# Attention and SwiGLU block on one core: the last unit's row sums on TensorE, the last output tiles split into FFN and attention, and a DMA ring in the scheduler's model

## The chip, the cores and the metric

One core of one Trainium2 chip. The metric is the device time of one execution in microseconds (us). All runs told here are of the fast state; a run also has a mean granted TensorE clock (1.000 is full speed).

Engine names: PE is TensorE's matmul, PEld its weight load, DVE is VectorE, ACT is ScalarE, POOL is GpSimd, SP issues the DMAs. "L1230" is a line of the kernel in question; lines of helpers collect many uses.

## The reference, cut to what matters

```python
def reference(A_x, A_wqkv, A_wo, B_x, B_w1, B_w3, B_w2):   # x: 1 x 2048 x 512, 32 heads of 16, F = 1792
    xn = _layernorm(A_x)
    q, k, v = split_heads(xn @ A_wqkv)
    p = softmax(q @ k.T * 16 ** -0.5)                       # 32 heads x 2048 x 2048 exponentials
    h = silu(xn @ B_w1) * (xn @ B_w3)
    return A_x + (p @ v) @ A_wo + h @ B_w2
```

## The kernel before: the parts that matter

The kernel writes its own schedule. While the program is built, a small simulator runs on the host with one clock per engine; whenever an engine is free *in the model*, the next piece of work is chosen and appended to that engine's instruction list. On the chip each engine runs its list in order, and semaphores keep it correct. So a wrong duration in the model does not make a wrong result by itself; it makes a wrong **order**, and an engine then stands before an instruction whose input is late while later work in its list could have run.

```python
class _Sched(_Prog):
    ...
    def dma(self, fn, reads=(), writes=(), kb=64, name="", eng="sp"):
        op = _Prog.dma(self, fn, reads, writes, name, eng)
        return self._time(op, op.deps, 0.06, 1.9 + kb / 200.0)     # 0.06 us to issue, no queueing
```

The work is 32 units (4 blocks of 512 queries x 8 groups of 4 heads). A unit has 64 score matmuls of 512 columns; most pairs of them are exponentiated by ACT (line `f_PT`, 128x1024), the others by a chain of DVE instructions (line `f_xd`). Dense tiles (Q, K, V, FFN, OUT) fill the gaps on PE. When a unit's P times V is complete, its sums of rows are inverted and spread over the partitions by DMA; the normalized result, `onorm`, is what the output tile (OUT) multiplies by A_wo:

```python
def unit_end(u, o):
    # e0: DVE copies U <- PSUM;  e1: DMA gathers the sums Lc <- U (and moves half of U)
    # e2: DVE Rc = 1 / Lc;       e3: DMA Rrow <- Rc
    # e4: 4 DMAs R <- Rrow, each row broadcast to 16 partitions
    # e5: onorm = U * R   (POOL; DVE for the last unit)
    ...
```

The output tile of the last query block had two parts: the FFN product with three of four attention groups (it can start only once the third group's onorm is there), and the last group by itself:

```python
def tile_OUT(tg, part):
    ...
    if part not in (2, 4): ... FFN groups ...
    for g in range(NP):
        if part == 1 and g == NP - 1 or part == 2 and g < NP - 1 or part == 3:
            continue
        ... attention group g ...
```

## Time and profile before

| | before |
|---|---|
| time, median of 3 runs (range) | 855.96 us (852.74 to 856.73) |
| span of the profiled run | 853.8 us |
| ACT busy, PE busy, DVE busy | 93%, 90%, 86% |
| ACT idle, 0 to 60 us | 24.1 us |
| last exponential to the end | 22.66 us |

Three lines of the page of the kernel before. The first has the busy time of each engine; the others are tenths of busy time of ACT, and tenths of the granted PE clock, in 40 slices of the span.

```profile
...
PE 764.9 (90%) x8693; PEld 214.3 (25%) x8693; DVE 738.3 (86%) x975; ACT 797.3 (93%) x893; POOL 30.9 (4%) x41
...
ACT  4589999999999999999999999999996999999990
...
PEclk9899999999999999999999999999996999999996
...
```
ACT is the bound nearly everywhere: it is at 9 in all slices but the first three (4, 5, 8), one in the middle (6) and the last (0). So time can only come back where ACT is idle. The stage table of the same kernel (from:to in us, length, busy us of each engine with the number of instructions, then the granted clock, the DMA share and GB/s):

```profile
...
core 0: us, PE busy (x) PEld busy (x) DVE busy (x) ACT busy (x) POOL busy (x), PEclk, DMA share, GB/s
26.00:40.00 14.00, 7.84 (x94) 2.94 (x90) 7.58 (x19) 7.78 (x9) 1.76 (x4) 0.87 0.64 184
40.00:60.00 20.00, 18.53 (x222) 5.46 (x214) 7.10 (x13) 15.63 (x17) 0.00 (x0) 0.92 0.06 14
640.00:644.00 4.00, 1.94 (x26) 0.41 (x18) 2.72 (x3) 2.88 (x4) 1.61 (x1) 0.98 0.26 13
644.00:650.00 6.00, 6.00 (x44) 1.03 (x46) 3.12 (x4) 3.36 (x4) 0.00 (x0) 0.50 0.06 22
650.00:657.00 7.00, 7.00 (x52) 1.20 (x44) 3.41 (x5) 4.83 (x5) 0.00 (x0) 0.50 0.06 19
831.14:853.80 22.66, 7.00 (x107) 2.72 (x99) 6.13 (x14) 0.00 (x1) 0.00 (x0) 0.66 0.28 41
...
```
Read it in three places. **Start**: from 40 to 60 us PE is busy 18.53 of 20 us, ACT has 4.4 us idle and DVE works only 7.1 us. **Dent**: from 644 to 657 us the clock is 0.50, PE is busy all the time, and ACT is idle 4.8 of 13 us (called a dip of the clock from here on); just before, in 640 to 644, PE was busy only 1.94 of 4 us. **Tail**: 22.66 us in which nothing is left for ACT.

Who stood waiting for whom (us in total, how often, the longest one), from the list of waits of the kernel before:

```profile
...
DVE f_onorm L1820 <- DMA f_R<-f_Rrow: 7.2, 1, 7.2
...
PE ps L1556 <- DMA f_KT<-f_stg: 6.0, 1, 6.0
...
PE ps L1230 <- POOL f_onorm L1820: 2.1, 1, 2.1
...
```
The first line is in the tail, the second in the start (at 33 to 39 us), the third is the one that precedes the dent. The tail itself, from the timeline (start, length, engine, line, operation, output and input, count; in brackets how long the engine was idle and what it waited for):

```profile
...
828.22 2.92 ACT L1594 ACTIVATE f_PT<-ps 128x1024 bf16<-128x1024 f32 x3
...
831.74 0.69 DVE L1778 COPY f_U<-ps 128x512 f32<-128x512 f32 x1 [3.42 <-PE ps L1760]
...
832.46 0.62 SPq L1785 DMA_DIRECT2D f_Lc<-f_U  x1
...
835.75 0.63 SPq L1805 DMA_DIRECT2D f_Rrow<-f_Rc  x1
...
837.80 2.42 SPq L1810 DMA_DIRECT2D f_R<-f_Rrow  x4
844.21 0.69 DVE L1820 TENSOR_TENSOR f_onorm<-f_U,f_R 128x512 bf16<-128x512 f32 x1 [7.22 <-DMA f_R<-f_Rrow]
...
844.96 1.90 PE L1230 MATMUL ps<-f_wo,f_onorm 128*32 128x512 bf16 x16 [8.72 <-DVE f_onorm L1820]
...
845.63 2.49 DVE L1428 TENSOR_TENSOR f_xn_sb<-ps,f_wkv 128x512 bf16<-128x512 f32 x4 [0.72 <-PE ps L1230]
...
846.35 3.10 SPq L1434 DMA_DIRECT2D out_dram<-f_xn_sb  x4
```
Follow the hops: last exponential ends at 831.14, U is copied, the sums are gathered by DMA (832.5 to 834.4), inverted, sent to Rrow (835.75 to 837.8), spread by four DMAs whose issue alone takes 2.4 us and which land at 844.1; DVE idles 7.22 us for them. PE, having stood still, runs the last 16 matmuls in 1.90 us.

### The profile page before, as it was taken

The numbers are of one execution on the slowest core, as the hardware profiler recorded it, in microseconds if no ns is written. First come the engines' busy times: TensorE is split into PE (matmuls) and PEld (weight loads), VectorE is DVE, ScalarE is ACT, GpSimd is POOL, SyncE is SP. The second block draws the span as 40 slices with busy tenths as digits, with TensorE's granted clock in tenths as the row PEclk, the third lists the DMA queues.
The fourth block names the chain that finished last, engine by engine and source line by source line (L and its number), as shares of the span: only waits on it lengthen the run. The fifth ranks groups of instructions, "written<-read, shape, count | busy, mean of one in ns | idle before, by whom it ended". The sixth has DMA issues, their size and how long they took to land.

```text
span 853.8 us, 20404 instructions
## 1 busy us (share of the span) xinstructions
PE 764.9 (90%) x8693; PEld 214.3 (25%) x8693; DVE 738.3 (86%) x975; ACT 797.3 (93%) x893; POOL 30.9 (4%) x41
## 2 busy tenths in 40 slices
PE   4689999998999999899999999899998989989892
PEld 2222222222222222222222222222221222222230
DVE  5548988999979989998999899998985899989982
ACT  4589999999999999999999999999996999999990
POOL 2100000000000000000000000000000000000000
PEclk9899999999999999999999999999996999999996
DMA  8503313233221223333211333333120432231222
GB/s 316 159 14 39 51 43 55 35 54 45 40 21 36 44 38 45 40 51 45 27 19 30 45 44 45 45 46 45 10 31 21 70 39 31 42 40 7 18 28 42
DMA packets 90580, 40.48 MB, mean 47 GB/s; under 512 B 72560, under 2 KB 86640, under 8 KB 90480
## 3 DMA queue, kind: packets, MB, share of 16 engines
q1 hardware_dynamic: 90480, 39.09, 29.4%
q8 instruction: 70, 1.15, 0.6%
q14 instruction: 30, 0.25, 0.1%
HBM read 22.81 MB, written 2.10 MB: 29 GB/s over the span
## 4 chain that ended last, share of the span: by engine, by line
ACT 64%; PE 21%; DVE 8%; DMA 5%; issue 1%; SPq 1%; POOL 0%; DVEq 0%; POOLq 0%
ACT f_PT L1594 61%; PE ps L1230 9%; PE ps L1556 7%; PE ps L1760 5%; ACT f_th L1366 3%; DVE f_xd L1646 2%; DMA f_KT<-f_stg 1%; DVE f_xd L1692 1%; DMA f_wkv<-in_A_wqkv_dram 1%; DMA f_R<-f_Rrow 1%; DVE f_xd L1706 1%; DVE f_xd L1685 1%; DVE f_hT L1380 1%; DMA f_QT<-f_stg 1%; DMA f_Rrow<-f_Rc 0%
## 5 line engine op out<-in xcount | busy, mean ns | idle before, releaser
L1594 ACT ACTIVATE f_PT<-ps 128x1024 bf16<-128x1024 f32 x819 | 769.2, 1095 | 19.4 <-PE ps L1556 18.6
L1556 PE MATMUL ps<-f_QT,f_KT 32*128 32x512 bf16 x2048 | 327.8, 388 | 40.4 <-ACT f_PT L1594 26.3
L1646 DVE TENSOR_SCALAR f_xd<-ps 128x1024 int16<-128x1024 f32 x205 | 250.3, 1221 | 32.1 <-PE ps L1556 24.2
L1760 PE MATMUL ps<-f_PT,f_Vaug 128*17 128x512 bf16 (+1 forms) x1638 | 223.1, 389 | 1.3 <-DVE f_xd L1701 0.6
L1760 PE MATMUL ps<-f_xd,f_Vaug 128*32 128x512 bf16 (+1 forms) x1230 | 178.9, 388 | 5.7 <-DVE f_xd L1692 2.2
L1556 PEld LDWEIGHTS ps<-f_QT,f_KT 32*128 32x128 bf16 x2048 | 82.0, 91 | 351.8 <-ACT f_PT L1594 301.1
L1230 PE MATMUL ps<-f_xnT,f_w 128*32 128x512 bf16 x1792 | 150.6, 383 | 8.0 <-DVE f_t L1370 5.9
L1692 DVE TENSOR_TENSOR f_xd<-f_xd 128x2048 bf16<-128x2048 bf16 (+1 forms) x112 | 126.2, 1127 | 0.0
L1701 DVE TENSOR_SCALAR f_xd<-f_xd 128x2048 int16<-128x2048 int16 (+1 forms) x112 | 74.1, 661 | 2.5
L1685 DVE TENSOR_SCALAR f_xd<-f_xd 128x2048 int16<-128x2048 int16 (+1 forms) x112 | 74.3, 663 | 2.1 <-PE ps L1760 0.2
L1706 DVE TENSOR_SCALAR f_xd<-f_xd 128x2048 int16<-128x2048 int16 (+1 forms) x112 | 74.2, 662 | 2.2
L1230 PE MATMUL ps<-f_w,f_hT 128*32 128x512 bf16 x896 | 75.8, 382 | 0.2 <-DVE f_wkv L1420 0.2
L1760 PEld LDWEIGHTS ps<-f_PT,f_Vaug 128*17 128x17 bf16 (+1 forms) x1638 | 54.2, 91 | 83.3 <-issue 69.1
L1760 PEld LDWEIGHTS ps<-f_xd,f_Vaug 128*32 128x32 bf16 (+1 forms) x1230 | 43.2, 92 | 56.1 <-issue 27.4
L1230 PEld LDWEIGHTS ps<-f_xnT,f_w 128*32 128x32 bf16 x1792 | 39.6, 95 | 59.2 <-issue 48.4
L1820 POOL TENSOR_TENSOR f_onorm<-f_U,f_R 128x512 bf16<-128x512 f32 x15 | 21.4, 1429 | 742.5 <-DMA f_R<-f_Rrow 647.9
L1370 DVE SCALAR_TENSOR_TENSOR f_t<-f_th,ps 128x512 bf16<-128x512 f32 x56 | 38.2, 682 | 8.8 <-ACT f_th L1366 8.6
L1380 DVE SCALAR_TENSOR_TENSOR f_hT<-f_t,ps 128x512 bf16<-128x512 bf16 x56 | 38.1, 681 | 6.1 <-PE ps L1230 4.9
L1366 ACT ACTIVATE f_th<-ps 128x512 f32<-128x512 f32 x56 | 38.9, 695 | 0.0
L1230 PE MATMUL ps<-f_wo,f_onorm 128*32 128x512 bf16 x256 | 24.9, 432 | 12.4 <-DVE f_onorm L1820 8.7
L1230 PEld LDWEIGHTS ps<-f_w,f_hT 128*32 128x32 bf16 x896 | 21.3, 95 | 19.9 <-issue 11.5
L1778 DVE COPY f_U<-ps 128x512 f32<-128x512 f32 x32 | 21.9, 684 | 4.1 <-PE ps L1760 4.0
(50 smaller groups left out, 210.1 us busy)
## 6 DMA issues: line engine op xcount, KB each, us to landing
f_w<-in_B_w_dram SPq DMA_DIRECT2D x112, 128.0 KB, 2.4
f_R<-f_Rrow SPq DMA_DIRECT2D x128, 32.0 KB, 4.0
f_KT<-f_hT SPq DMA_DIRECT2D x6, 512.0 KB
f_KT<-f_stg SPq DMA_DIRECT2D x32, 64.0 KB, 2.0
f_QT<-f_stg SPq DMA_DIRECT2D x32, 64.0 KB
f_U<-f_U SPq DMA_DIRECT2D x64, 32.0 KB, 2.0
f_xr<-in_A_x_dram SPq DMA_DIRECT2D x16, 128.0 KB
out_dram<-f_xn_sb SPq DMA_DIRECT2D x16, 128.0 KB, 3.3
```

The source lines that it names most:

```text
L1230: ins = e.matmul(bank(bk)[32 * i:32 * i + 32, 0:ncols], make_lhsT(i), rhs_ap, start=start, stop=stop, tile_position=(0, 32 * i))
L1366: q = P.op("act", lambda e: e.activation(th[:, ss, :], bank(bk), ACTF.Tanh, scale=0.5), reads=[("ps", bk)], writes=[("th", ss)], dur=a_cos ...
L1370: q2 = P.op("dve", lambda e: e.scalar_tensor_tensor(t1[:, ss, :], th[:, ss, :], 1.0, bank(bk), ALU.add, ALU.mult), reads=[("th", ss), ("ps ...
L1380: q = P.op("dve", lambda e: e.scalar_tensor_tensor(hT[:, fc, :], t1[:, ss, :], 0.5, bank(bk), ALU.mult, ALU.mult), reads=[("t1", ss), ("ps ...
L1556: ins = e.matmul(bank(b), l_, r_, start=True, stop=True, tile_position=(rp, 0))
L1594: q = P.op("act", lambda e: e.activation(PT[:, s_, :], ps[:, b0 * 512:(b0 + 2) * 512], ACTF.Exp, scale=ASC, bias=ABIAS), reads=[("ps", b0) ...
L1646: q = P.op("dve", lambda e: e.tensor_scalar(dsl[:, ys, 1024 * c:1024 * c + 1024], ps[:, 4 * 512:6 * 512], 0.0, 32767.0, ALU.max, ALU.min), ...
L1685: P.op("dve", lambda e: e.tensor_scalar(dsl[:, NY + m_, 0:n], y, 0x7F, 0x3F00, ALU.bitwise_and, ALU.bitwise_or), reads=[("ds", ys)], write ...
L1692: q_ = P.op("dve", lambda e: e.tensor_tensor(t_ap.bitcast(BF16), y.bitcast(BF16), t_ap.bitcast(BF16), ALU.mult), reads=[("ds", ys)], write ...
L1701: q_ = P.op("dve", lambda e: e.tensor_scalar(g_ap, y, -352.0, 0.0, ALU.add, ALU.max), reads=[("ds", ys)], writes=[("ds", NY + NM + g_)] + ...
L1706: q_ = P.op("dve", lambda e: e.tensor_scalar(y, y, 0x7F80, None, ALU.bitwise_and), reads=[], writes=[("ds", ys)], dur=s_cost(n), name="e")
L1760: ins = e.matmul(bank(PV)[32 * j:32 * j + (17 if g % 2 == 0 else 32), :], v_, p_, start=s0, stop=s1, tile_position=(0, 32 * j))
```

## The change

The intent, in four pieces. (1) The **last** unit's sums are taken by fp32 matmuls from the copied U, inverted out of PSUM by DVE, and spread by 16 small fp32 matmuls with an identity. (2) The last pair's onorm comes in two halves, each masked, A (the first unit of the pair, still by DMA, multiplied by DVE while the scores still run) and B (by TensorE), and the last OUT becomes FFN alone (early) plus attention alone (five groups, late). Odd tiles add the FFN sum by an fp32 matmul with the identity, so that ACT can take their last copy. (3) The DMA model: 0.56 us per issue, one ring that all DMAs share at 270 KB per us, 1.5 us to land. (4) Small matters: constants made on POOL, bank 5 kept free at the end, four open tiles at the end instead of two.

```diff
-    def dma(self, fn, reads=(), writes=(), kb=64, name="", eng="sp"):
+    def dma(self, fn, reads=(), writes=(), kb=64, name="", eng="sp", rate=270.0):
         op = _Prog.dma(self, fn, reads, writes, name, eng)
-        return self._time(op, op.deps, 0.06, 1.9 + kb / 200.0)
+        self._time(op, op.deps, 0.56, 0.0)
+        self.ring = max(self.ring, op.end) + kb / rate
+        op.end = self.ring + 1.5
+        return op
 ... (constants idf, sell, msk) ...
 def tile_OUT(tg, part):
+            gr = {2: ats + [og(NP - 1, ON_B, ("ON", qc, "B"))], 3: ffn, 4: ats, 0: ffn + ats}[part]
+            by_pe = part == 2 and ts % 2 == 1
+            if by_pe:
+                groups.insert(1, (lambda e, bk: e.matmul(bank(bk), idf[:, :], osum[:, ts, :], start=False, stop=False),
+                                  [("idf",), ("osum", ts)], None, 0.95))
 ...
             for ts in range(4):
-                bg.append(tile_OUT(sc * 4 + ts, 1 if sc == NQC - 1 else (3 if sc < 3 else 0)))
+                bg.append(tile_OUT(sc * 4 + ts, 3))
 ...
 def unit_end(u, o):
-                if h:
-                    eng = "dve" if u == NU - 1 else "pool"
+                if h or u == NU - 2:
+                    eng = "dve" if u == NU - 2 else "pool"
 ...
+        def last_end(o):
+            # ACT: U <- PSUM;  PE: 4 matmuls U.T @ sell (the sums);  DVE: reciprocal from PSUM
+            # PE: 16 matmuls, Rc broadcast x identity (the spread);  DVE: onorm B = U * mask * PSUM
```

More of the change, by code (lines that the diff above doesn't have):

```diff
@@ L149, in __init__ @@
         self.t = 0.0
+        self.ring = 0.0
     def _time(self, op, deps, dur, tail):
@@ L1072, in _plan_fast @@
         fm = sb("fm", [1, 1], FP32)
+        idf = sb("idf", [128, 128], FP32)
+        sell = sb("sell", [128, 4], FP32)
+        msk4 = sb("msk4", [128, 4], FP32)
+        msk = sb("msk", [128, 2], FP32)
         def bank(b):
@@ L1206, in _plan_fast, with tail_consts, tail_masks @@
         P.post("dve", wv_check, ready=60.0, prio=4)
+        def tail_consts():
+            P.op("pool", lambda e: e.memset(idf[:, :], 1.0), writes=[("idf",)], dur=0.2)
+            P.op("pool", lambda e: e.affine_select(idf[:, :], idf[:, :], [[1, 128]], ALU.is_equal, 0.0,
+                                                   base=0, channel_multiplier=-1),
+                 reads=[("idf",)], writes=[("idf",)], dur=0.4)
+            P.op("pool", lambda e: e.memset(sell[:, :], 1.0), writes=[("sell",)], dur=0.1)
+            P.op("pool", lambda e: e.affine_select(sell[:, :], sell[:, :], [[-32, 4]], ALU.is_equal, 0.0,
+                                                   base=-15, channel_multiplier=1),
+                 reads=[("sell",)], writes=[("sell",)], dur=0.2)
+            P.op("pool", lambda e: e.memset(msk4[:, :], 1.0), writes=[("msk4",)], dur=0.1)
+            P.op("pool", lambda e: e.affine_select(msk4[:, :], msk4[:, :], [[-32, 4]], ALU.is_ge, 0.0,
+                                                   base=-16, channel_multiplier=1),
+                 reads=[("msk4",)], writes=[("msk4",)], dur=0.2)
+            P.op("pool", lambda e: e.affine_select(msk4[:, :], msk4[:, :], [[32, 4]], ALU.is_ge, 0.0,
+                                                   base=31, channel_multiplier=-1),
+                 reads=[("msk4",)], writes=[("msk4",)], dur=0.2)
+            P.post("dve", tail_masks, ready=P.free["pool"] + _LAT, prio=4)
+        def tail_masks():
+            P.op("dve", lambda e: e.tensor_reduce(msk[:, 1:2], msk4[:, :], AX.X, ALU.add), reads=[("msk4",)],
+                 writes=[("msk", 1)], dur=0.1)
+            P.op("dve", lambda e: e.tensor_scalar(msk[:, 0:1], msk[:, 1:2], -1.0, 1.0, ALU.mult, ALU.add),
+                 reads=[("msk", 1)], writes=[("msk", 0)], dur=0.1)
+        P.post("pool", tail_consts, ready=100.0, prio=4)
         def load_w13(idx):
@@ L1396, in tiles_FFN, with og @@
                     _T("Y%d_%d" % (sc, fc), mk(1), evac_u, cond=lambda: ("G%d_%d" % (sc, fc)) in done)]
+        ON_B = (NQC * NP) % NON
         def tile_OUT(tg, part):
             qc, ts = divmod(tg, 4)
-            gr = []
-            if part not in (2, 4):
-                for fc in range(FC):
-                    gr.append((lambda i, fc=fc: hT[:, fc, ts * 128 + 32 * i:ts * 128 + 32 * i + 32], w2[:, fc, :],
-                               [("hT", fc), ("w2",)], None))
-            for g in range(NP):
-                if part == 1 and g == NP - 1 or part == 2 and g < NP - 1 or part == 3:
-                    continue
-                gr.append((lambda i, g=g: onorm[:, (qc * NP + g) % NON, ts * 128 + 32 * i:ts * 128 + 32 * i + 32], wo[:, g, :],
-                           [("ON", (qc * NP + g) % NON)] + [("wor", j_, h_) for j_ in range(4) for h_ in range(2)],
-                           lambda g=g: have(("ON", qc, g))))
+            def og(g, slot, key):
+                return (lambda i: onorm[:, slot, ts * 128 + 32 * i:ts * 128 + 32 * i + 32], wo[:, g, :],
+                        [("ON", slot)] + [("wor", j_, h_) for j_ in range(4) for h_ in range(2)],
+                        lambda: have(key))
+            ffn = [(lambda i, fc=fc: hT[:, fc, ts * 128 + 32 * i:ts * 128 + 32 * i + 32], w2[:, fc, :],
+                    [("hT", fc), ("w2",)], None) for fc in range(FC)]
+            ats = [og(g, (qc * NP + g) % NON, ("ON", qc, g)) for g in range(NP)]
+            gr = {2: ats + [og(NP - 1, ON_B, ("ON", qc, "B"))], 3: ffn, 4: ats, 0: ffn + ats}[part]
+            by_pe = part == 2 and ts % 2 == 1
@@ L1412, in tile_OUT @@
             groups = []
             for k, (lh, rh, rd, cd) in enumerate(gr):
-                groups.append((lambda e, bk, lh=lh, rh=rh, k=k: col_groups(lh, rh, D)(e, bk, k == 0, k == len(gr) - 1),
-                               rd, cd, DG))
+                groups.append((lambda e, bk, lh=lh, rh=rh, k=k: col_groups(lh, rh, D)(
+                    e, bk, k == 0, k == len(gr) - 1), rd, cd, DG))
+            if by_pe:
+                groups.insert(1, (lambda e, bk: e.matmul(bank(bk), idf[:, :], osum[:, ts, :], start=False, stop=False),
+                                  [("idf",), ("osum", ts)], None, 0.95))
@@ L1417, in evac, with e1 @@
             def evac(bk, o, rel):
-                def e1():
-                    if part in (1, 3):
+                def e1(eng="dve"):
+                    if part == 3:
                         q = P.op("dve", lambda e: e.tensor_tensor(osum[:, ts, :], bank(bk), xr[:, ts % 2, :], ALU.add),
@@ L1427, in e1 @@
                     other = osum[:, ts, :] if part in (2, 4) else xr[:, ts % 2, :]
-                    q = P.op("dve", lambda e: e.tensor_tensor(osb[:, ts, :], bank(bk), other, ALU.add),
+                    if by_pe and eng == "act":
+                        fn = lambda e: e.activation(osb[:, ts, :], bank(bk), ACTF.Identity)
+                    elif by_pe:
+                        fn = lambda e: e.tensor_copy(osb[:, ts, :], bank(bk))
+                    else:
+                        fn = lambda e: e.tensor_tensor(osb[:, ts, :], bank(bk), other, ALU.add)
+                    q = P.op(eng, fn,
                              reads=[("ps", bk), ("osum", ts) if part in (2, 4) else ("xr", ts % 2)],
                              writes=[("osb", ts), ("xn", ts)],
-                             dur=d_cost(512))
+                             dur=d_cost(512) if eng == "dve" else a_cost(512))
                     rel(q)
@@ L1436, in e1 @@
                            ready=q.end + _LAT, prio=1)
-                P.post("dve", e1, ready=o.end + _LAT, prio=1, cond=lambda: part in (2, 4) or ("xr", tg) in done)
+                if by_pe:
+                    P.post2({"dve": lambda: e1("dve"), "act": lambda: e1("act")}, ready=o.end + _LAT,
+                            prios={"dve": 2, "act": 1})
+                else:
+                    P.post("dve", e1, ready=o.end + _LAT, prio=1, cond=lambda: part in (2, 4) or ("xr", tg) in done)
             def cond():
-                if part in (2, 4):
+                if part == 4:
                     return have(("OSUM", tg), ("ON", qc, NP - 1))
+                if part == 2:
+                    return have(("OSUM", tg)) and st["pos"] >= NR
                 if not have(*[("hT", qc, fc) for fc in range(FC)]):
                     return False
-                if part in (1, 3) and qc > 0 and ("OUT", (qc - 1) * 4 + ts) not in done:
+                if part == 3 and qc > 0 and ("OUT", (qc - 1) * 4 + ts) not in done:
                     return False
@@ L1447, in cond @@
                     return have(*[("KTm", NG - 1, i_) for i_ in range(NQC)])
-                g_need = NP - 2 if part == 1 else NP - 1
-                return have(("ON", qc, g_need))
+                return have(("ON", qc, NP - 1))
             def start():
@@ L1516, in dense_banks @@
             if st["pos"] >= NR and st["n_exp"] >= NR:
-                return [6, 0, 1, 2, 3, 4, 5]
+                return [6, 0, 1, 2, 3, 4]
             if st["early"]:
@@ L1795, in ec @@
                     l_check(0, NU - 1, 1)
-                elif u == NU - 1:
-                    done["accb"] = l_check(NU - 1, NU, 2).end + _LAT
             def e2():
@@ L1819, in e5 @@
                 on = (u // 2) % NON
+                if u == NU - 2:
+                    q = P.op(eng, lambda e: e.scalar_tensor_tensor(onorm[:, on, :], U[:, 0, :], msk[:, 0:1], R[:, :],
+                                                                   ALU.mult, ALU.mult),
+                             reads=[("Uc",), ("msk", 0)] + [("R", j_, h_) for j_ in range(4) for h_ in range(2)],
+                             writes=[("ON", on)], dur=0.68)
+                    done[("ON", qc, pi)] = q.end + _LAT
+                    return
                 q = P.op(eng, lambda e: e.tensor_tensor(onorm[:, on, :], U[:, 0, :], R[:, :], ALU.mult),
@@ L1825, in e5, with copy, col_sums, f @@
                 done[("e5", u // 2)] = q.end
+            if u == NU - 1:
+                return last_end(o)
             P.post("dve", e0, ready=o.end + _LAT, prio=0, cond=lambda: u < 2 or h == 1 or ("e5", u // 2 - 1) in done)
+        def last_end(o):
+            u = NU - 1
+            qc = NQC - 1
+            def copy():
+                q = P.op("act", lambda e: e.activation(U[:, 1, :], bank(PV), ACTF.Identity), reads=[("ps", PV)],
+                         writes=[("Ut",)], dur=a_cost(512), name="U")
+                st["tail"] = (q.end + _LAT, col_sums)
+            def col_sums():
+                def f(e):
+                    for k in range(4):
+                        ins = e.matmul(bank(5)[:, 4 * k:4 * k + 4], U[:, 1, 128 * k:128 * k + 128], sell[:, :],
+                                       start=True, stop=True)
+                    return ins
+                q = P.op("pe", f, reads=[("Ut",), ("sell",)], writes=[("ps", 5)], dur=0.6, name="S")
+                P.post("dve", inv, ready=q.end + _LAT, prio=0)
+            def inv():
+                q = P.op("dve", lambda e: e.reciprocal(Rc[:, :], bank(5)[:, 0:16]), reads=[("ps", 5)],
+                         writes=[("Rc",)], dur=0.25)
+                st["tail"] = (q.end + _LAT, spread)
+                P.op("dve", lambda e: e.tensor_copy(Lc[:, u, :], bank(5)[:, 0:16]), reads=[("ps", 5)],
+                     writes=[("Lc", u)], dur=0.1)
+                done["accb"] = l_check(NU - 1, NU, 2).end + _LAT
+            def spread():
+                def f(e):
+                    for k in range(4):
+                        for j in range(4):
+                            ins = e.matmul(bank(PV)[32 * j:32 * j + 32, 128 * k:128 * k + 128],
+                                           Rc[:, 4 * k + j:4 * k + j + 1].to_broadcast((128, 32)), idf[:, :],
+                                           start=True, stop=True, tile_position=(0, 32 * j))
+                    return ins
+                q = P.op("pe", f, reads=[("Rc",), ("idf",)], writes=[("ps", PV)], dur=1.1, name="S")
+                P.post("dve", norm_b, ready=q.end + _LAT, prio=0)
+            def norm_b():
+                q = P.op("dve", lambda e: e.scalar_tensor_tensor(onorm[:, ON_B, :], U[:, 1, :], msk[:, 1:2], bank(PV),
+                                                                 ALU.mult, ALU.mult),
+                         reads=[("Ut",), ("ps", PV), ("msk", 1)], writes=[("ON", ON_B)], dur=0.68)
+                done[("ON", qc, "B")] = q.end + _LAT
+            P.post("act", copy, ready=o.end + _LAT, prio=0)
@@ L1832, in start_tile @@
             banks = [b for b in dense_banks() if bank_free[b] <= P.t and not any(a.bank == b for a in active)]
-            if not banks or len(active) >= 2:
+            if not banks or len(active) >= (4 if st["pos"] >= NR else 2):
                 return
@@ L1844, in start_tile @@
                 tl = None
-                cand = bg[:3] + [x for x in bg[3:] if x.name[0] == "O" and x.name.endswith("_4")]
+                cand = bg[:4 if st["pos"] >= NR else 3] + [x for x in bg[3:] if x.name[0] == "O" and x.name.endswith("_4")]
                 if cand and any(z[0] == 0 for z in crit[:4]):
@@ L1893, in fin @@
         def fin():
-            o = P.op("pe", lambda e: e.matmul(bank(PV)[:, 0:3], ones_t[:, :], accb[:, :], start=True, stop=True),
-                     reads=[("ones_t",)] + [("acc", i) for i in range(3)], writes=[("ps", PV)], dur=0.1)
+            o = P.op("pe", lambda e: e.matmul(bank(5)[:, 0:3], ones_t[:, :], accb[:, :], start=True, stop=True),
+                     reads=[("ones_t",)] + [("acc", i) for i in range(3)], writes=[("ps", 5)], dur=0.1)
             def f1():
-                P.op("dve", lambda e: e.tensor_reduce(fm[:, :], bank(PV)[0:1, 0:3], AX.X, ALU.min),
-                     reads=[("ps", PV)], writes=[("fm",)], dur=0.1)
+                P.op("dve", lambda e: e.tensor_reduce(fm[:, :], bank(5)[0:1, 0:3], AX.X, ALU.min),
+                     reads=[("ps", 5)], writes=[("fm",)], dur=0.1)
                 P.op("dve", lambda e: e.tensor_scalar(flag[:, :], fm[:, :], 127.5, None, ALU.is_lt),
@@ L1914, in _plan_fast @@
                 if P.free["pe"] <= P.t:
-                    if not st["fin"] and have("accb"):
+                    if st.get("tail") and st["tail"][0] <= P.t:
+                        f_ = st["tail"][1]
+                        st["tail"] = None
+                        f_()
+                        moved = True
+                    elif not st["fin"] and have("accb"):
                         fin()
```

## The prediction

> **What bounds the kernel now.** The page: ACT busy 93% of 853.8 us, PE 90%, DVE 86%. The stage table: ACT is at least 99% busy from 60 to 620 us and from 660 to 831 us. So exponentials bound the main loop, and time comes back only where ACT idles: 0-60 us (about 24 us idle), a dent at 640-657 us (6.5 us idle) and the tail from 831.2 us (last exponential) to 853.8 us (22.6 us).
>
> **Three places where the change acts.**
>
> 1. Tail. The timeline after 831.7: U copied by DVE 0.7; sums by DMA 832.5 to 834.4; reciprocal; Rrow DMA 835.75 to 837.8; four R issues 2.4 and landing at 844.1; onorm 844.2 to 844.9; last matmuls, at half clock, to 846.9; adds to 848.1; four output issues 846.35 to 849.45; end 853.8. The chain of waits names DMA and its issue from 835.7 to 844.1. After: U copy on ACT (est. 0.6), fp32 sum matmuls and their latency (about 1), reciprocal from PSUM 0.3, fp32 spread matmuls (1.2-2), norm_b 0.7. A fp32 product is four passes (Trainium skill, "FP8 and Floating Point Precision", TensorE Precision Notes); no fp32 matmul is in this trace, so these are estimates from 0.215 us per group of four bf16 matmuls. The second half of onorm is then ready near 836, not 845. PE meanwhile has the 16 groups of the attention part (3.5 us) and two fp32 adds of osum (near 1 us each); this nearly fits and keeps the clock up. FFN matmuls of the last OUT, 4.5 us of which lie in the tail now, can start near 785 rather than 796, where PE idles 2.4 us in 10. The 7 us from last matmul to end stay nearly whole. Gain 8 us (5-11).
>
> 2. Dent at 640. PE waited 2.06 us for onorm, because four R issues took 6.4 us from first issue to landing, where the old schedule model thinks 2.3. Clock fell to 0.61 until 657 and ACT lost 6.5 us. (Trainium skill, "TensorE: Matmul & The Clock Gate", What's actually happening: an idle array goes to half clock; here 2 us of waiting sufficed.) The new model charges 0.56 per issue and 1.5 after the ring: about 3.9, so the tile should start later and not block. Gain 5 (0-7).
>
> 3. Start. The old model thinks all inputs land by 5 us (real: 12.4) and K packs in 2.2 us (real 9.7, queued behind 2.8 MB of late loads). PE so waited 6 us (33-39), with transposes and K/V tiles stuck behind; from 40 to 60 PE was the limit (18.5 of 20) while ACT idled 4.4 and DVE worked 7.1 of 20; first DVE exponential at 60.9. With the ring, those tiles should run during the wait and DVE should begin near 40-50. First score may slip 1-3 us. Gain 5 (-2 to 9).
>
> The whole program is rescheduled; I expect under 2 us of that either way.
>
> **Prediction.** 856 - 8 - 5 - 5 = 838, less a little for mishaps: 840 us, range 832-850. Faster by over 2% (under 839): 0.43; within 2%: 0.55; slower: 0.02.
>
> **Right if the profile shows:** no R DMA in the last 20 us, last exponential to end near 14.5 us; PE waits for onorm gone from the middle, clock 1.0 throughout; PE wait for K pack below 3 us, DVE exponentials from before 50 us; ACT busy about 790.
>
> **Wrong if:** fp32 matmuls with their weight loads take several us; K packs queue still later, so the first scores slip; the model, still 2.5 us optimistic about R, makes a new block and clock dip elsewhere; the order change costs DVE its share of exponentials.

## The result

| | before | after |
|---|---|---|
| time, median | 856.35 us (4 runs, 852.74 to 857.43) | 841.77 us (4 runs, 840.42 to 842.33) |
| ratio of the fast runs, 95% interval | | 0.9838 (0.9808 to 0.9868) |
| span of the profiled run | 853.8 us | 838.6 us |
| ACT idle, 0 to 60 us | 24.1 us | 17.9 us |
| last exponential to the end | 22.66 us | 16.24 us |

Ratios here and below are those of the fast runs of one kernel against the kernel before in the same rounds, so they are not quite the ratio of the medians.

The page after:

```profile
...
PE 764.4 (91%) x8769; PEld 215.5 (26%) x8769; DVE 746.1 (89%) x986; ACT 797.7 (95%) x898; POOL 31.0 (4%) x48
...
ACT  4799999999999999999999999999999999999993
...
PEclk9999999999999999999999999999999999999998
...
```
ACT's busy time is the same (797.7 us against 797.3); its share rose because the span shrank. The stages (columns as before):

```profile
...
26.00:40.00 14.00, 12.58 (x172) 4.91 (x160) 7.34 (x17) 11.73 (x16) 1.43 (x3) 1.00 0.71 206
40.00:60.00 20.00, 17.65 (x210) 4.88 (x214) 16.72 (x22) 18.75 (x21) 0.00 (x0) 1.00 0.06 14
640.00:657.00 17.00, 16.21 (x188) 4.39 (x184) 16.46 (x24) 16.54 (x19) 0.00 (x0) 1.00 0.14 41
822.36:838.60 16.24, 8.44 (x115) 3.99 (x111) 3.05 (x10) 1.68 (x3) 0.00 (x0) 0.84 0.13 39
...
```
In 26 to 40 us PE is busy 12.58 us where it was 7.84; in 40 to 60 DVE is busy 16.72 us where it was 7.10; in 640 to 657 the clock is 1.00. The waits that answer to those shown before:

```profile
...
DVE f_onorm L1867 <- DMA f_R<-f_Rrow: 2.7, 1, 2.7
...
PE ps L1263 <- POOL f_onorm L1873: 0.3, 1, 0.3
...
```
The wait of PE for a K pack is gone from the list; that for onorm is 0.3 us instead of 2.1. But the first line has moved: DVE waits 2.7 us for R **in the body**, at 808 to 811 us, where it used to wait in the tail. The tail:

```profile
...
817.42 4.93 ACT L1642 ACTIVATE f_PT<-ps 128x1024 bf16<-128x1024 f32 x5
...
822.95 1.12 PE L1450 MATMUL ps<-f_wkv,f_idf 128*128 128x512 f32 x2
823.06 0.60 ACT L1888 ACTIVATE f_U<-ps 128x512 f32<-128x512 f32 x1 [0.71 <-PE ps L1808]
...
824.99 1.06 PE L1895 MATMUL ps<-f_sell,f_U 128*128 128x4 f32 x8
...
826.63 1.05 PE L1913 MATMUL ps<-f_idf,f_Rc 128*32 128x128 f32 x32
...
827.75 0.75 DVE L1921 SCALAR_TENSOR_TENSOR f_onorm<-f_U,f_msk,ps 128x512 bf16<-128x512 f32 x1 [0.76 <-PE ps L1913]
...
828.05 1.12 PE L1450 MATMUL ps<-f_wkv,f_idf 128*128 128x512 f32 x2
...
829.10 1.69 PE L1263 MATMUL ps<-f_wo,f_onorm 128*32 128x512 bf16 x28
830.20 1.29 DVE L1469 TENSOR_TENSOR f_xn_sb<-ps,f_wkv 128x512 bf16<-128x512 f32 x2 [1.47 <-PE ps L1263]
830.42 1.08 ACT L1465 ACTIVATE f_xn_sb<-ps 128x512 bf16<-128x512 f32 x2 [6.76 <-PE ps L1263]
830.92 2.61 SPq L1476 DMA_DIRECT2D out_dram<-f_xn_sb  x4
```
There is no DMA between the last exponential and the outputs. PE is now the engine that is busy nearly all the way from 822.95 to 830.8.

Progress can be compared point by point, because all kernels issue the same 2048 score matmuls in the same order. The time at which the first one of a unit starts (taken from the traces, by counting score matmuls; us):

| | before | after | after minus before |
|---|---|---|---|
| unit 0 | 25.21 | 30.46 | +5.3 |
| unit 1 | 66.52 | 58.64 | -7.9 |
| unit 8 | 240.03 | 233.67 | -6.4 |
| unit 24 | 627.59 | 620.78 | -6.8 |
| unit 25 | 658.94 | 646.03 | -12.9 |
| unit 31 | 806.50 | 795.23 | -11.3 |
| last score | 829.69 | 820.90 | -8.8 |
| end | 853.8 | 838.6 | -15.2 |

So in this pair of traces: the start gives 7.9 us (6 to 7 of it stay), the unit with the dent 6.1, the last unit **takes back** 2.5, the tail gives 6.4.

### The profile page after: what moved, and what is told of

Same layout as the page of the kernel before. It is cut to its first block, busy times and chain, and to the rows that moved or that the text cites. A ratio compares the mean times of both kernels' runs of the same rounds, so it can differ in the third digit from the quotient of the medians.

```text
span 838.6 us, 20568 instructions
## 1 busy us (share of the span) xinstructions
PE 764.4 (91%) x8769; PEld 215.5 (26%) x8769; DVE 746.1 (89%) x986; ACT 797.7 (95%) x898; POOL 31.0 (4%) x48
## 4 chain that ended last, share of the span: by engine, by line
ACT 66%; PE 18%; DVE 11%; DMA 2%; issue 1%; SPq 0%; ACTq 0%; DVEq 0%
ACT f_PT L1642 63%; PE ps L1263 8%; PE ps L1604 5%; PE ps L1808 4%; DVE f_xd L1694 4%; ACT f_th L1399 3%; DVE f_xd L1740 2%; DVE f_xd L1749 1%; DVE f_xd L1733 1%; DMA f_wkv<-in_A_wqkv_dram 1%; DVE f_xd L1754 1%; DVE f_t L1403 1%; DVE f_hT L1413 1%; DMA f_R<-f_Rrow 1%; PE ps L1291 0%
## 5 line engine op out<-in xcount | busy, mean ns | idle before, releaser
L1642 ACT ACTIVATE f_PT<-ps 128x1024 bf16<-128x1024 f32 x815 | 764.5, 1103 | 10.2 <-PE ps L1604 9.5
L1604 PE MATMUL ps<-f_QT,f_KT 32*128 32x512 bf16 x2048 | 325.8, 386 | 34.7 <-ACT f_PT L1642 28.4
L1694 DVE TENSOR_SCALAR f_xd<-ps 128x1024 int16<-128x1024 f32 x209 | 255.0, 1220 | 32.1 <-PE ps L1604 24.0
L1808 PE MATMUL ps<-f_PT,f_Vaug 128*32 128x512 bf16 (+1 forms) x1630 | 221.7, 387 | 2.2 <-DVE f_U L1826 0.6
L1808 PE MATMUL ps<-f_xd,f_Vaug 128*17 128x512 bf16 (+1 forms) x1254 | 180.3, 384 | 9.9 <-DVE f_xd L1749 4.0
L1740 DVE TENSOR_TENSOR f_xd<-f_xd 128x2048 bf16<-128x2048 bf16 (+1 forms) x115 | 130.2, 1132 | 0.0
L1733 DVE TENSOR_SCALAR f_xd<-f_xd 128x2048 int16<-128x2048 int16 (+1 forms) x115 | 76.7, 667 | 2.2 <-PE ps L1263 0.2
L1754 DVE TENSOR_SCALAR f_xd<-f_xd 128x2048 int16<-128x2048 int16 (+1 forms) x115 | 76.3, 664 | 2.2
L1749 DVE TENSOR_SCALAR f_xd<-f_xd 128x2048 int16<-128x2048 int16 (+1 forms) x115 | 73.8, 642 | 2.5
L1808 PEld LDWEIGHTS ps<-f_PT,f_Vaug 128*32 128x32 bf16 (+1 forms) x1630 | 53.8, 91 | 81.5 <-issue 64.9
L1808 PEld LDWEIGHTS ps<-f_xd,f_Vaug 128*17 128x17 bf16 (+1 forms) x1254 | 43.5, 92 | 63.5 <-issue 27.2
L1263 PE MATMUL ps<-f_xnT,f_wq 128*32 128x512 bf16 x256 | 23.2, 383 | 0.0
L1263 PE MATMUL ps<-f_wkv,f_xnT 128*32 128x512 bf16 x256 | 19.2, 421 | 3.8 <-DMA f_wkv<-in_A_wqkv_dram 3.7
```

The lines of the kernel that those rows point to most:

```text
L1263: ins = e.matmul(bank(bk)[32 * i:32 * i + 32, 0:ncols], make_lhsT(i), rhs_ap, start=start, stop=stop, tile_position=(0, 32 * i))
L1604: ins = e.matmul(bank(b), l_, r_, start=True, stop=True, tile_position=(rp, 0))
L1642: q = P.op("act", lambda e: e.activation(PT[:, s_, :], ps[:, b0 * 512:(b0 + 2) * 512], ACTF.Exp, scale=ASC, bias=ABIAS), reads=[("ps", b0) ...
L1694: q = P.op("dve", lambda e: e.tensor_scalar(dsl[:, ys, 1024 * c:1024 * c + 1024], ps[:, 4 * 512:6 * 512], 0.0, 32767.0, ALU.max, ALU.min), ...
L1733: P.op("dve", lambda e: e.tensor_scalar(dsl[:, NY + m_, 0:n], y, 0x7F, 0x3F00, ALU.bitwise_and, ALU.bitwise_or), reads=[("ds", ys)], write ...
L1740: q_ = P.op("dve", lambda e: e.tensor_tensor(t_ap.bitcast(BF16), y.bitcast(BF16), t_ap.bitcast(BF16), ALU.mult), reads=[("ds", ys)], write ...
```

## The experiments

The theory: three gains from separate causes (start and dent from the model, tail from TensorE), less new waits, of which the DVE wait for R is the largest. Rivals: all in the tail; all in the reordering; or the dent an accident. All runs were correct unless said.

### Ring model alone

```diff
 # kernel before, only:
-        return self._time(op, op.deps, 0.06, 1.9 + kb / 200.0)
+        self._time(op, op.deps, 0.56, 0.0)
+        self.ring = max(self.ring, op.end) + kb / rate
+        op.end = self.ring + 1.5
 ... (return op, rate=270.0, self.ring = 0.0) ...
```

> The kernel before with nothing but the new DMA model in the scheduler (0.56 us per issue, one ring at 270 KB/us, 1.5 us to land). Theory (three separate gains: start about 6 us, tail about 6.4 us, dent at 640 us about 6 us, less about 4 us of new waits): this run has start and dent but the old tail, so 845 to 849 us against 856; ACT idle before 60 us near 18 instead of 24; from the last exponential to the end still 22 to 23 us; PE wait for onorm in the middle under 0.5 us. Rival A (the gain is nearly all in the tail, and the schedule change is worth nothing in sum): 854 to 857. Rival B (nearly all from the schedule): 842 to 844.

Measured: 846.46 us (6 runs, 842.57 to 849.03), ratio 0.9892 (0.9866 to 0.9918). ACT idle before 60 us 17.3 us, last exponential to end 23.4 us, no PE wait for onorm. As the theory said: about two thirds of the gain needs no change to the tail.

### Tail alone

```diff
 # changed kernel, with the old dma():
 ... (the four new lines out) ...
+        return self._time(op, op.deps, 0.06, 1.9 + kb / 200.0)
```

> The changed kernel with the old DMA model: tail by TensorE and split OUT alone. Theory: tail 16 to 17 us instead of 22.6, start as before (ACT idle near 24 us to 60 us, first DVE exponential near 61), and the DVE half of the norm (placed on DVE now) waits longer for R than in the changed kernel, because the old model thinks R lands 1.6 us earlier: 3 to 5 us of DVE idle there, 2 to 4 us of ACT idle. So 850 to 854. If the dent at 640 comes from the optimistic model and not from chance, it is here too (PE wait for onorm about 2 us, clock near 0.6 for 10 us). Rival A (all in the tail): 842 to 846. Rival B: 855 to 858.

Measured: 851.78 us (6 runs, 850.16 to 856.24), ratio 0.9964 (0.9939 to 0.9989). Last exponential to end 17.7 us, ACT idle before 60 us 23.7. Waits of this run:

```profile
...
DVE f_onorm L1864 <- DMA f_R<-f_Rrow: 4.2, 1, 4.2
...
PE ps L1260 <- POOL f_onorm L1870: 2.1, 1, 2.1
...
```
Both predicted waits are here: DVE stands 4.2 us before R (2.7 with the ring), ACT loses 5.5 us between 800 and 831 us, and PE waits 2.1 us for onorm. But the half clock after that wait is **not** here: unit 24 took 25.7 us (31.4 in the first trace of before, with the same wait). The wait is the model's; the dip is not bound to it. A dip does follow the other wait: DVE's ends at 817.0 us, and the clock is at half from 819.7 to 833.4 us.

The product of the two ratios, ring alone (0.9892) and tail alone (0.9964), is 0.9856; the change has 0.9838. Within the intervals the two halves add. (The tail alone holds both the split and the sums on TensorE; the runs below take these apart.)

### Ring model only until 60 us

```diff
 # changed kernel, in dma():
+        if not (self.t < 60.0):
+            return self._time(op, op.deps, 0.06, 1.9 + kb / 200.0)
```

> The changed kernel, new DMA model only for DMAs issued before 60 us of schedule time, the old one afterwards. Start and tail gains kept. Theory (the accurate model removes the wait at 640): the wait for onorm comes back somewhere in the middle, with a clock dip, and the DVE wait for R grows: 845 to 850. Rival (the dent was an accident of one order, the model after 60 us is worth nothing): 840 to 843, no PE wait for onorm above 1 us.

Measured: 846.37 us (6 runs, 843.71 to 849.86), ratio 0.9883 (0.9862 to 0.9903), against 0.9838 for the change. Its waits:

```profile
...
DVE f_onorm L1869 <- DMA f_R<-f_Rrow: 3.4, 1, 3.4
...
PE ps L1265 <- POOL f_onorm L1875: 2.7, 1, 2.7
...
```
The wait of PE for onorm is back, at another place (249 us; unit 8 took 27.4 us instead of 22.4), and the DVE wait is longer. In this trace the clock was 0.52 from 250 to 256 us, so here a dip followed the wait; another, from 819.0 to 832.7 us, followed the DVE wait, and the last unit took 30.2 us instead of 25.7. The trace is that of the slowest of the six runs. On the medians the model after 60 us is worth some 4 us; the rival falls.

### A later onorm in the model of the kernel before

```diff
 # kernel before, in e5():
-                done[("ON", qc, pi)] = q.end + _LAT
+                done[("ON", qc, pi)] = q.end + _LAT + (3.0 if eng == "pool" else 0.0)
```

> The kernel before, with only the time at which the scheduler believes an onorm from Pool is ready moved 3 us later (waits on the chip are unchanged; only the order of PE work moves). Theory (the dent at 640 is a PE queue blocked by an optimistic model): no PE wait for onorm above 0.5 us, PE clock 1.0 from 640 to 660, that unit of scores 25 to 26 us instead of 31, 848 to 852 us. Rival (the dent is chance and comes back elsewhere): 854 to 857.

Measured: 858.84 us (6 runs, 852.98 to 859.68), ratio 1.001 (0.9983 to 1.0037). The profiled run did what the theory said at that place (no PE wait for onorm, clock 1.00 from 640 to 657, unit 24 in 25.3 us, 6.0 us earlier than the first trace of before at unit 25), and was one of the two quick runs, 853 us. The other four took 859. Even in the quick trace the clock fell to 0.50 to 0.57 from 786 to 798 us, in another unit (unit 30: 27.3 us against 24.3). So the rival is right about the price: removing this one wait in this way bought **nothing** on the median. The fastest and the slowest run are also those with the highest and the lowest mean granted clock: 852.98 us at 0.984, 859.68 at 0.970.

### The kernel before once more

```diff
 # no edit
```

> The kernel before once more, for a second trace. If the half clock after the PE wait for onorm at 642 us is bound to that wait, the dip is here too and that unit of scores takes about 31 us. If the dip depends on where the wait falls in some window of the clock control (the run of the tail alone had the same wait of 2.1 us and no dip), the wait of 2 us is here but the dip may be absent or another length: 26 to 31 us.

Measured: 855.57 us (2 runs), ratio 0.9983. The wait of 2.1 us is there again, the dip is shorter (0.68 and 0.79 in two stages of 6 and 7 us) and the unit took 28.4 us, between the 25.7 of the tail alone and the 31.4 of the first trace. The same instruction list, two prices. Part of the 5 us and more by which runs of one kernel differ may come about in this way; the spans of these two traces do not differ so (853.8 and 854.7 us), and the second has more dips elsewhere.

### The split alone

```diff
 # ring model alone, plus:
-                if part == 1 and g == NP - 1 or part == 2 and g < NP - 1 or part == 3:
+                if part == 3:
                     continue
-                bg.append(tile_OUT(sc * 4 + ts, 1 if sc == NQC - 1 else (3 if sc < 3 else 0)))
+                bg.append(tile_OUT(sc * 4 + ts, 3))
 ... part 2 may start when the scores are all issued; four open tiles at the end ...
```

> The kernel before with the new DMA model (846.5 us in the run of ring only) plus the split of the last OUT (FFN part early, all four attention groups late), the row sums still by DMA hops. Theory: the chain of DMA hops, 12 us from the last U copy to the norm, bounds the tail, and the leftover FFN matmuls (4 us on PE) are hidden under it; so the split alone is worth nothing: 844.5 to 848, last exponential to end 22 to 24 us. Rival (the split is a gain of its own, since the FFN leaves the tail): 840 to 843.

Measured: 841.87 us (6 runs, 840.09 to 846.48), ratio 0.9824 (0.978 to 0.9867). **The expectation was wrong in the sum and right about the tail**: last exponential to end is 23.2 us, as without the split, yet the median is 4.6 us better than with the ring alone (the rounds were others; ratios 0.9824 and 0.9892). The stages tell where. Ring alone (old split), 772 to 792 us:

```profile
...
772.00:780.00 8.00, 6.41 (x52) 1.25 (x53) 7.76 (x10) 7.88 (x9) 0.00 (x0) 0.84 0.09 18
780.00:786.00 6.00, 5.95 (x42) 1.11 (x40) 3.65 (x4) 5.60 (x7) 0.67 (x1) 0.50 0.65 44
786.00:792.00 6.00, 6.00 (x51) 1.10 (x50) 4.55 (x5) 4.19 (x5) 0.60 (x1) 0.57 0.01 3
...
```
The split, same stages:

```profile
...
772.00:780.00 8.00, 8.00 (x101) 2.10 (x94) 7.79 (x11) 8.00 (x10) 0.00 (x0) 1.00 0.10 21
780.00:786.00 6.00, 6.00 (x74) 1.77 (x78) 5.53 (x7) 6.00 (x8) 0.00 (x0) 1.00 0.63 62
786.00:792.00 6.00, 5.79 (x74) 1.46 (x66) 5.83 (x8) 5.73 (x7) 1.27 (x1) 1.00 0.02 6
...
```
Without the split no dense tile may run between the end of the FFN and the third onorm, so PE has holes (6.41 busy of 8), the clock goes to one half, and ACT then loses 1.8 us in the third stage. With the split the FFN part of OUT fills the holes and the clock stays. The holes themselves cost ACT next to nothing (it is busy 7.88 of 8 there); the loss comes with the low clock. How small they are, from the timeline of PE with the ring alone:

```profile
...
773.43 0.39 PE L1560 MATMUL ps<-f_QT,f_KT 32*128 32x512 bf16 x4 [0.53 <-ACT f_PT L1598]
...
775.26 0.39 PE L1560 MATMUL ps<-f_QT,f_KT 32*128 32x512 bf16 x2 [0.53 <-ACT f_PT L1598]
...
777.10 0.39 PE L1560 MATMUL ps<-f_QT,f_KT 32*128 32x512 bf16 x4 [0.53 <-ACT f_PT L1598]
...
```
Gaps of 0.53 us, one in 1.83 us; the clock falls at 777.5. That the whole difference of the medians comes from this is not shown; the two traces differ by 2.9 us in the span. But ACT and POOL have the same list of instructions in both kernels, those of PE and DVE differ only from unit 30 on, and up to there the two traces run alike: ring alone has one dip of 3.4 us, at 477 us, and is still 0.6 us ahead at the start of unit 30 (767.94 against 768.54). Unit 30 then takes 27.8 us against 24.5.

Read against the change, this run says more: ring and split alone, with the old sums by DMA, have the time of the whole change (841.87 us, 0.9824, against 841.77, 0.9838). In the traces the sums on TensorE shorten the tail by 7.0 us (23.2 to 16.2), but the last unit is 2.8 us longer (25.7 against 22.9) and unit 31 starts 2.2 us later. So on the medians the first piece of the change paid nothing as it stood; it pays once the DVE wait is mended (837.88 and 836.13 us below).

### Sums by TensorE, without the split

```diff
 # changed kernel:
-            gr = {2: ats + [og(NP - 1, ON_B, ("ON", qc, "B"))], 3: ffn, 4: ats, 0: ffn + ats}[part]
+            gr = {1: ffn + ats[:NP - 1], 2: [ats[NP - 1], og(NP - 1, ON_B, ("ON", qc, "B"))], 3: ffn, 4: ats, ...}[part]
-                bg.append(tile_OUT(sc * 4 + ts, 3))
+                bg.append(tile_OUT(sc * 4 + ts, 1 if sc == NQC - 1 else 3))
 ... (the conditions of part 1) ...
```

> The changed kernel (841.8 us) without the split: the last OUT is FFN plus three attention groups in one part and the fourth group with the two halves in the other, as before; sums by TensorE kept. Theory: with the DMA hops gone PE is the bound of the tail (busy from 822.9 to 830.8 in the changed kernel), so the 4 us of FFN leftover come onto the path, less the 2.6 us of attention groups that move out of the tail: 842 to 845, tail 17 to 20 us. Rival (the split does not matter, PE has slack): 840 to 842.

Measured: 842.53 us (6 runs, 840.17 to 846.48), ratio 0.9833 (0.9791 to 0.9875): not to be told from the change (0.9838). The tail is 17.1 us, 0.9 longer than with the split. So with the new tail the split brings under 1 us of tail. And this trace shows the other side of the clock: here PE had the same holes at 772 to 786 us (5.98 of 8, 4.64 of 6) with the clock at 1.00, and a dip to 0.50 at 812 to 818, after the DVE wait. So the holes do not always bring a dip, and with the new tail a gain from the split is not shown.

### First half of the last norm on POOL

```diff
 # changed kernel: e5 of the unit before the last
-                    eng = "dve" if u == NU - 2 else "pool"
+                    eng = "pool"
-   scalar_tensor_tensor(onorm, U, msk, R)                 # DVE
+   tensor_scalar(R, R, msk, mult); tensor_tensor(onorm, U, R, mult)   # POOL
```

> The changed kernel with the first-half norm of the last pair on Pool (a multiply of R by the mask and the old product) instead of DVE. Theory: the DVE wait of 2.7 us for R near 808 to 811 and the ACT gaps of about 2 us at 812 to 816 go; 838.5 to 840.5 against 841.8 for the changed kernel. Rival (those ACT gaps come from something else, or a stall turns up elsewhere): 841 to 844.

Measured: 837.88 us (6 runs, 835.14 to 840.31), ratio 0.9791 (0.9766 to 0.9815). The DVE wait is gone, ACT idle from 800 us to the last exponential is 0.4 us instead of 2.2, and the last unit's scores take 23.4 us (last score minus unit 31) instead of 25.7.

### R later in the model

```diff
 # changed kernel, in e4(), after each of the four DMAs R <- Rrow:
+                    q.end += 2.5
```

> The changed kernel with 2.5 us added in the model to the landing of the spread R (the model says about 3.9 us for four issues and landing, the trace 6.4). Norm of the first half stays on DVE. Theory (the block of DVE at 808 to 811 comes from the model's optimism about R): DVE wait for R under 0.5 us, ACT gaps at 812 to 816 gone, 838.5 to 840.5. Rival (moving the norm off DVE is what helped in the run with Pool, not its time): 841 to 843.

Measured: 836.13 us (6 runs, 835.34 to 839.25), ratio 0.9761 (0.9721 to 0.9801). The norm stays on DVE and costs nothing now, because the model places it after R has landed. The changed kernel, 806 to 818 us:

```profile
...
806.00:812.00 6.00, 5.27 (x66) 1.29 (x58) 3.22 (x5) 6.00 (x8) 0.00 (x0) 1.00 0.61 41
812.00:818.00 6.00, 5.07 (x56) 1.44 (x56) 5.79 (x8) 3.99 (x5) 0.00 (x0) 1.00 0.02 3
...
```
With R later in the model:

```profile
...
806.00:812.00 6.00, 6.00 (x82) 1.69 (x74) 5.85 (x7) 6.00 (x8) 0.00 (x0) 1.00 0.36 32
812.00:818.00 6.00, 5.47 (x68) 1.48 (x64) 3.81 (x5) 6.00 (x7) 0.00 (x0) 1.00 0.01 4
...
```
ACT is busy 12.0 of 12 us instead of 10.0. So it was the time of that instruction in DVE's list, not its place on DVE: two mends, one result. The last unit's scores, over all runs, sort by this one thing: DVE norm placed by the optimistic model 25.7 (the change), 28.1 (no split) and 27.9 (the next run); on POOL 23.4; placed by the mended model 23.0; with the old tail and the ring, where there is no such instruction, 23.2 and 22.9. The clock sets part of this price too: the waits of DVE are alike in the first three (2.7, 2.5 and 2.8 us), but after it the clock stayed full in the trace of the change and was at half for 6.8 and 10.2 us in the other two.

### No fp32 adds on PE

```diff
 # changed kernel:
-            by_pe = part == 2 and ts % 2 == 1
+            by_pe = False
```

> The changed kernel without the two fp32 matmuls that add osum on PE (1.06 us each in its trace); all four last sums by DVE. Theory (PE bounds the tail): sums, spread and second half about 1 us earlier, last matmul about 2 us earlier, of which four adds in a row on DVE (0.6 each) give back about 1: tail 15 to 15.7 us, 840.3 to 841.3. Rival (the sharing of the adds between ACT and DVE is worth its matmuls): 842 to 843.5, tail 16.5 to 17.5.

Measured: 838.94 us (6 runs, 834.46 to 840.14), ratio 0.9776 (0.9734 to 0.9818). Last exponential to end is 13.9 us instead of 16.2. The tail gains more than expected (2.4 instead of 0.5 to 1.2 us): two fp32 adds of 1.06 us each leave PE's path, and the last copies on one engine take 2.48 us where two engines shared them in 1.3 us. How the rest comes about is not taken apart.

### Both mends together

```diff
 # changed kernel with  q.end += 2.5  and  by_pe = False
```

> Two mends together: R 2.5 us later in the model (836.1 us alone) and no fp32 adds on PE (tail 13.9 instead of 16.2 alone). If they add: last score near 816, tail 13.5 to 14.5, 833 to 835 us. If the tail of the first is bound by something else: 835.5 to 837.

Measured: 836.47 us (5 runs, 833.65 to 838.4), ratio 0.9754 (0.973 to 0.9777). Tail 14.6 us (13.5 to 14.5 expected), but the body of the profiled run was 3.3 us later than with R alone at the last score, with a dip at 692 us. This version beats both kernels, 2.5% under the kernel before and, by the ratios, 0.8% under the change; but R later alone (836.13 us, 0.9761) is as good, and that the second mend adds to the first is not shown.

### The ring without the cost of an issue

```diff
 # changed kernel, in dma():
-        self._time(op, op.deps, 0.56, 0.0)
+        self._time(op, op.deps, 0.06, 0.0)
```

> The changed kernel with the ring kept in the model but 0.06 us per issue instead of 0.56. Theory (in the start it is the shared ring, several MB of loads ahead of the K packs, that matters): ACT idle before 60 us stays near 18 us and unit 1 of the scores starts at 58 to 60. But R is then modelled about 2 us earlier, so waits of PE for onorm of 1.5 to 3 us return and the DVE wait for R grows to about 4.5: 844 to 850. Rival (the issue cost makes the start gain): unit 1 at 64 to 67, ACT idle 22 to 24.

Measured: 853.54 us (6 runs, 849.47 to 855.2), ratio 0.9952, and the **result was wrong** (relative error 0.67), which was not meant. We do not know why; an order of instructions should not be able to do this, so some dependency that the kernel does not record, or does not need in its usual orders, is likely, but that is a guess. With that caution: ACT idle before 60 us is 16.5 us and unit 1 starts at 58.1, so, as far as a run with a wrong result can say it, the start gain needs the ring and not the issue cost; and the waits grew as expected (PE for onorm 2.7 us, DVE for R 4.6 us). It was slower than expected.

## Why the prediction was right or wrong

**The sum.** 841.77 us was measured, 840 predicted, range 832 to 850; within 2% was the likelier side and it is what came (ratio 0.9838). The terms behave differently from the sum, and that the sum lies so near is partly luck: in the traces the start gave more than its 5 us (7.9, of which 6.4 stay), the tail less than its 8 (6.4), and a loss of 2.5 us in the last unit stood in no term. Nor do the pieces of the change stand for the terms: ring and split with the old sums had the same time (841.87 us).

**Start, predicted 5 us (-2 to 9): right, mechanism and size.** The scores of unit 1 start 7.9 us earlier and 6.4 remain at unit 8. As predicted, PE no longer waits for the K pack, transposes and V tiles run in its place (PE 12.58 of 14 us busy in 26 to 40, before 7.84), and the first DVE exponential is at 42.1 us instead of 60.9. The first score slipped by 5.3 us, more than the 1 to 3 said: before, PE waited 1.66 us for its pack; after, there is no such wait, and other tiles stand before it in the list (that the model now has this pack land later is the likely reason, not a tested one). Part of what PE had lost before was clock: in the wait of 6 us a dip began, from 36.2 to 43.1 us, and after the change the clock is 1.00 there. The ring alone shows the gain; the last experiment above, with its caution, says that it is the shared ring and not the issue.

**Dent, predicted 5 us (0 to 7): the wait right, its price mis-read.** Five traces whose model takes R, and so onorm, to be earlier than the change's does (before twice, tail alone, ring until 60 us, no issue cost) have a PE wait for onorm of 2.1 to 2.7 us; the others made with the ring have 0.3 or none. That part is the model. But the 6 us in the trace of before were mostly half clock (ACT idle 4.8 us in 644 to 657, 1.1 in 640 to 644), and the same wait of 2.1 us cost units of 31.4, 28.4 and 25.7 us in three traces. Taking the wait away without anything else (onorm 3 us later) changed the median by nothing; in the one trace of it, a quick run, the clock dipped elsewhere (786.9 to 800.5 us). The prediction read one trace's dip as the price of its wait. What the new model after 60 us is worth in sum was measured by leaving it out: 846.4 against 841.8 us, some 4 us, in onorm waits and in the length of the DVE wait.

**Tail, predicted 8 us (5 to 11): right in kind, the PE term mis-sized.** Predicted last exponential to end "near 14.5 us", measured 16.24. The prediction said that PE's extra work "nearly fits". It does not: PE is busy from 822.95 to 830.8, the second half of onorm is ready 6.1 us after the last exponential (828.5) instead of about 5, and without the two fp32 adds the tail is 13.9. A single fp32 product of 128x512 took 1.06 us (0.95 in the scheduler's model, "near 1" in the prediction); the sum of them on a full engine was the error. Trainium skill, "FP8 and Floating Point Precision", TensorE Precision Notes, gives four passes for true fp32; here the trace lists two PE instructions for each fp32 matmul, 1.06 us together against 0.215 for a group of four bf16 ones that makes a product of the same size: 4.9 times, somewhat more than the four passes.

**A term that the sum had only as a risk.** "The model, still 2.5 us optimistic about R, makes a new block elsewhere": it did, on DVE, since the change itself put the norm of the first half into DVE's list while that list still carries exponentials; POOL, which makes the norms of the other pairs, could have waited without harm, as the run with the norm on POOL shows. It cost 2.3 to 2.7 us in the last unit of the profiled run, where the clock stayed full, and near 5 us in the two traces where a dip followed (28.1 and 27.9 us against 23.0 to 23.4). Mending it either way, by place or by model, gave back 4 to 5.6 us on the medians (ratios 0.9791 and 0.9761 against 0.9838).

**Missed in detail.** ACT busy stayed at 797.7 us, not 790; the clock was not 1.0 throughout (at half for 3.4 us at 137 us and again at 690 us). That the FFN can leave the tail was right but is worth under 1 us there; with the old tail the split paid where it kept PE filled at 772 to 792 us, which the prediction saw ("PE idles 2.4 us in 10") without seeing the clock behind it; with the new tail the run without it was as fast (842.53 us).

## What to carry to other kernels

Where a program is scheduled on a host's model, look in the trace for the engine that stands before a late input and compare the model's latency of that one input with the measured one; a mend of 2.5 us in one constant gave 5.6 us on the medians, where this whole change gave 14.6. Keep an instruction that waits for a DMA out of the list of an engine that the main loop needs, or place it there by the measured latency. And count small PE holes as a risk even where PE is not the bound: their price is the clock, it differs from run to run, and one trace can neither show nor refute it.

## What the Trainium skill lacked or had wrong

- "TensorE: Matmul & The Clock Gate", HAM oscillation, gives as the abstract rule no PE gaps over about 3.4 us. Here the clock fell to 0.50 within a single wait of 2.06 us (at 643.8 us before). Its "What's actually happening" calls the window free-running, and that agrees: the same wait of 2.06 us in the tail-alone trace was followed by no dip, and all dips but the last one of each trace, which runs into its end, last 3.41 us or two, three or four times that.
- "DMA: Bandwidth & Descriptors", Anatomy of one DMA — SWDGE (gpsimd) path, fits about 2.0 us fixed plus bytes over 436 GB/s. The fit is for DMAs issued by GpSimd; carried over to the DMAs of SP here, it gives as an estimate 2.1 us for 32 KB and 2.3 us for four such together. The four 32 KB DMAs that spread one partition's row to 16 partitions each took 6.3 us from the first issue to the last landing (837.8 to 844.1 us before). The formula has no term for a source of few partitions, and that section points to none. "SBUF — State Buffer", Door 1: The DMA port swizzle, has one: 27.6 GB/s measured for partitions 0..3 (transfers of 1 MiB), where these rows lie; as an estimate 128 KB over 27.6 GB/s plus the 2.0 us is 6.7 us, close to the measured 6.3. That the port is the cause here is not tested by any run.
